# Packed attention and an ELU feed-forward: leftover tokens kept raw, the value product turned, the order set anew

## The chip, the core and the metric

The kernel runs on one core of a Trainium2 chip. The metric is the device time of one execution in microseconds, the median over the timed runs; lower is better.

## The reference

Eight batches of 576 tokens with 8 heads of 64. First 32 packed queries `p` of each head attend to all keys and values; then the 576 queries `q` attend to the 32 packed rows, which serve as keys and as values. The result, 4608 tokens of 512, goes through a feed-forward layer with 2048 hidden units and ELU, all in float32:

```python
p_packed = sm_attn(p, k, v)
out = sm_attn(q, p_packed, p_packed)          # (8, 8, 576, 64) -> x: (4608, 512)
h = x @ w_in
g = np.where(h > 0.0, h, alpha * (np.exp(np.minimum(h, 0.0)) - 1.0))
return (g @ w_out).astype(np.float32)
```

## The kernel before

**Attention of a batch** (`attention`, from line 430). The heads go in four pairs with two heads `g` each; the packed rows of a pair lie in a strip of 32 columns (`cols_of`). TensorE makes the scores (`s1`, L539; L580 in two halves from batch 3 on), DVE takes the row maximum, ACT the exponential with the row sum, and TensorE turns the result 128 columns at a time (`tr1`, L650) so that ACT or DVE can copy it to SBUF as `e1T`. The value product `pv` (L676) then has `e1T` as the stationary operand, 32 columns for each head, and the values, 64 columns, streaming past it; it writes 32 partitions x 64. ACT or DVE scale the rows by the reciprocal sum (`norm`, L688 and L690), TensorE turns the 128x128 result once more (`tr2`, L702), and a copy makes `ppT`, the packed rows with the head dimension on the partitions. `ppT` feeds both the second scores (`s2`, L721) and the products with `w_in` (`mstep`, L822), so that the hidden layer is computed as attention weights times (packed rows times `w_in`).

**Numbers in two words.** A float32 product (L676, L721, L822, L1321) runs in the trace as two passes on TensorE, each with its own load of the stationary operand (PEld) and its own stream (PE). A product of split operands (`a_hi`, `a_lo`, `m_hi`, `m_lo`, `g`, `wo_a`, `wo_b`, `sw`: high word and remainder) is three passes, one for each of three pairings of words, that stream at a faster rate. `H_PLAIN = [0, 1]` lets the first quarter of the hidden layer of batches 0 and 1 use float32 as it is (L1321); all other hidden products are split (L1328, L1059).

**Hidden layer and output.** A batch has two windows of tokens: 256 tokens, and 320 of which 64 are "left over", since output tiles are 128 tokens. ACT makes `relu(-h)` and its exponential, DVE the ELU. The 64 left over tokens of every batch have their ELU made at once (`hb`, written by L1066 and L1344), go to DRAM (`rest_dram`), and are multiplied with `w_out` beside the last batch, 256 of them at a time (`strassen_pair` with `rest`). Batches 0 and 1 go through the output product in `VISITS`, pieces of a window's 16 hidden blocks; each visit ends with two accumulators copied out and stored, added in DRAM by the POOL queue where the rows were stored before. From batch 2 on two hidden blocks are taken together, with Strassen's scheme for the 2x2 blocks: 7 products of 256 columns, 3 passes each (21 passes of L1215), for which DVE makes sums (`sums`, L1141) and weight sums `sw` come from DRAM. `S_PLAINS` names the pairs that are multiplied without it: 4 products of 512 columns, 12 passes of L1215 (where the list of a window lacks pair 0, two of 512 and four of 256, 18 passes).

**What sets the order.** The program is written out by a planner (`schedule`): every piece of work is an `op` with an urgency, a duration for each engine that may do it, the work it needs and the buffers that it takes. The planner goes through time, gives the most urgent ready op to a free engine, and the instructions are then written in that order, one list for each engine. The engines follow their lists, with semaphores for what they need. Where the planner sees TensorE idle in the start-up it puts in matmuls whose result nobody reads (`fill`, L185). Loads are issued by SP's queue in the planned order. `kvq` has two buffers for each batch's keys, values and queries in turn, so that the queries of a batch are loaded once its value product has run.

Of the kernel before, what the change touches and what calls it, by code (L numbers as in the profile page):

```python
# [23 lines left out]
def packed_attention_elu_ffn(  # L24
# [23 lines left out]
    B, P, NPAIR, S = qT.shape  # L48
# [16 lines left out]
    LATE = 1.5  # L65
# [18 lines left out]
    ]  # L84
    T_ATT = [5.5, 0.5, 17.0, 10.0, -5.5, 16.0]
    T_ATT1 = [-22.0, -10.5, -21.5, -13.5, -21.5, -9.0]
    LI = 3.5
    LO = 1.5
    LM = 1.5
    LOOK = 4.0  # L90
    TM = [25.5, 32.5, 37.0, 33.5]
    FIRST = "i2 k q v i1 i3 i0".split()
    T_FILL = 1.5
    T_S2 = -21.0
    STAY = 15
    SWITCH = 0.105
    F_PLAIN = 0
    H_PLAIN = [0, 1]
    T_WS = 7
    T_AS = 3  # L100
# [5 lines left out]
    T_SW7 = 33  # L106
    T_ATTS = {3: [0.5, -1.5, -9.5, -3.0, 11.0, 21.5], 4: [-7.0, 4.5, 13.0, 5.0, 9.5, 23.0], 5: [-5.5, 2, -16.5, -2.5, 12.5, 28.0], 6: [5, 7.5, 13.5, 1.5, 11.5, 24.5], 7: [1.0, -13, 3.0, -3.0, 9.5, 23.0]}
    TMS = {3: [18, 27.0, 35.0, 30.5], 4: [21.5, 19.5, 26.0, 33.0], 5: [12.5, 28.5, 29.0, 29.5], 6: [23, 14.5, 24.0, 27.5], 7: [16.5, 35.5, 32.5, 29.0]}
    T_RL = -3.0
    T_RX = 0.5  # L110
    T_HS = 41.5
    S_FIRST = (2, 0)
    T_SW = 14.0
    T_SL = 6.0
    T_SE = 18.0
    LOOK_S = 5.5
# [70 lines left out]
    def schedule():  # L187
# [8 lines left out]
        todo = sorted(ops, key=lambda o: (o.prio, o.n))  # L196
        idle_at = {e: 0.0 for e in GAP}
        now, out, mode, converted, dense = 0.0, [], None, 0, 0.0
        conv = set(conv_ops)

        def engine_for(o):

            if o.wait or o.ready > now:
# [9 lines left out]
        while todo:  # L213
            for n, o in enumerate(todo[:400]):
                if o.wait or o.ready > now:
                    continue
# [3 lines left out]
                if e == "PE" and o.mode != mode and mode is not None:  # L220

                    for x in todo[n:n + 400]:
                        if x.mode == mode and x.prio < o.prio + STAY and engine_for(x) == "PE":
                            o = x
                            break
# [8 lines left out]
                o.start, o.end = now, now + cost + LAG[e] + o.lag  # L234
                for x, needs in o.next:
                    x.wait -= 1
                    if needs:
                        x.ready = max(x.ready, o.end + x.late)
                for r in {id(b.ring): b.ring for b in o.take}.values():
                    r.take([b for b in o.take if b.ring is r], now)  # L240
                out.append((o, e))
                todo.remove(o)
                converted += o in conv
                break
            else:
                if fill_end.end is None and now >= T_FILL and idle_at["PE"] <= now:
# [11 lines left out]
                    idle_at["PE"] = o.end  # L258
                    out.append((o, "PE"))
                    continue  # L260
                ends = [o.end + t for o, _ in out[-700:] for t in (0, LATE) if o.end + t > now]
                ends += [t for t in idle_at.values() if t > now]
                assert ends, [(o.prio, o.on) for o in todo[:20]]
                now = min(ends)
# [32 lines left out]
    nc.vector.memset(ebias, -1023.0 * LN2)  # L297
    warm = const.tile([P, 1], F32, name="warm")
# [138 lines left out]
    def attention(b, ts):  # L437
# [13 lines left out]
        pp_b = ring_tile("pp", small, [P, G, D], F32, "pp", bufs=1)  # L451
# [25 lines left out]
        def queries(pair, half):  # L477
            if b == 0:
                return q_b[0].t[:, pair, half * HS:(half + 1) * HS]
# [26 lines left out]
        def load_q(e, n):  # L506
            if b == 0:
                nc.sync.dma_start(out=q_b[0].t, in_=qT[b])
            else:
                nc.sync.dma_start(  # L510
                    out=q_b[n].t[:, :NPAIR * HS].rearrange("p (c s) -> p c s", c=NPAIR),
                    in_=qT[b, :, :, n * HS:(n + 1) * HS],
                )

        lds, prev_ld = {}, prev_b and prev_b.ld_q
        for name, fn, bufs, t in (
# [3 lines left out]
            if b == 0:  # L520
                t = FIRST.index(name) - 60
            for n, x in enumerate(bufs):
                prev_ld = op(
                    t, {"DMA": (3.3 if b < 3 else 3.8) / len(bufs)}, lambda e, fn=fn, n=n: fn(e, n),
                    take=[x] + ([p_b] if (name, n) == ("k", 0) else []), after=[prev_ld],
                    lag=1.5 * (b > 2),
# [85 lines left out]
        o4s, o, t, free = [], None, ts[0], prev_b.tmp_last if b > 1 else None  # L612
# [29 lines left out]
        for g in range(G):  # L642
# [23 lines left out]
            tr_done += [o7, o8]  # L666
            e1T.append(eT)
        ps = banks(2)

        def pv(e, ps=ps):  # L670
            for c in range(NKC):
                n = min(P, S - c * P)
                for g in range(G):
                    for pair in range(NPAIR):
                        h = 2 * pair + g
                        nc.tensor.matmul(  # L676
                            ps.t[cols_of(pair), g, :D],
                            lhsT=e1T[g].t[:n, c, cols_of(pair)],
                            rhs=values(c, h)[:n],
                            start=(c == 0), stop=(c == NKC - 1),  # L680
                        )

        o = op(ts[2], {"PE": 1.28}, pv, ld_v + tr_done, take=[ps, pp_b], use=v_b + e1T, mode=2)
        done = []
        for g in range(G):
            def norm(e, g=g, ps=ps):
                if e == "ACT":
                    nc.scalar.mul(pp_b.t[:, g, :], ps.t[:, g, :D], sv["ri"][:, g:g + 1])  # L688
                else:
                    nc.vector.tensor_scalar(  # L690
                        out=pp_b.t[:, g, :], in0=ps.t[:, g, :D], scalar1=sv["ri"][:, g:g + 1],
                        scalar2=None, op0=ALU.mult,
                    )

            done.append(op(
                ts[2], {"ACT": 0.25, "DVE": 0.27}, norm, [o, o5] + done,
                use=[ps, pp_b],
            ))
        pt2 = banks(1)

        def tr2(e, ps=pt2):
            nc.tensor.transpose(  # L702
                out=ps.t[:, :P], in_=pp_b.t.rearrange("p g d -> p (g d)"), identity=ident
            )

        def tr2c(e, ps=pt2):
            copy(e, st.ppT.t.rearrange("p c i -> p (c i)"), ps.t[:, :P])

        o = op(ts[3], {"PE": 0.06}, tr2, done, take=[pt2, st.ppT], use=[pp_b])
        st.ppT_op = op(ts[3], {"ACT": 0.27, "DVE": 0.29}, tr2c, [o], use=[pt2, st.ppT])  # L710
        st.a_done, st.af_done = [], []
        prev = []
        for half in range(2):
# [69 lines left out]
            o = op(t, {"PE": 0.52}, s2, [lds["q"][half % len(q_b)], st.ppT_op],  # L783
# [753 lines left out]
```

## Time and profile before

| | before |
|---|---|
| median of 3 runs | 700.87 us (699.53 to 701.19) |
| profiled execution | 700.24 us, span 698.2 us |
| TensorE busy | 686.1 us, 98% of the span |
| VectorE busy | 573.6 us, 82% |
| ScalarE busy | 455.3 us, 65% |
| granted TensorE clock | 0.998 |
| DMA | 167.80 MB, mean 240 GB/s |

Streams on TensorE overlap at their ends, so one row's duration is longer than the distance to the next row. The chain of waits counts each piece of TensorE work from the start of its first pass to the start of what follows; that is the time that it takes of the engine. "x80" there means 80 passes.

### The profile page before, as it was taken

What the parts mean: (1) busy time and instruction counts of PE and PEld (TensorE: products, weight loads), DVE (VectorE), ACT (ScalarE), POOL (GpSimd) and SP (SyncE); (2) the same over time, 40 slices, a digit from 0 to 9 for tenths busy, and PEclk for the clock granted to TensorE, in tenths of its full rate; (3) what the DMA queues carried; (4) which work ended last, traced back from release to release, by engine and by line L of the source; (5) the groups of instructions that cost most, each with busy time, mean ns of one, the idle gap of its engine ahead of it and who ended that gap; (6) DMA issues with size and microseconds to landing.
All of it is one profiled execution on the core that took longest, in us unless ns stands there. A gap on an engine that the chain in (4) does not pass through costs nothing.

```text
span 698.2 us, 16294 instructions
## 1 busy us (share of the span) xinstructions
PE 686.1 (98%) x6197; PEld 604.8 (87%) x6197; DVE 573.6 (82%) x1282; ACT 455.3 (65%) x888; POOL 21.1 (3%) x30
## 2 busy tenths in 40 slices
PE   8989999999999999999999999999999999999996
PEld 6766878887879989998989988898889988999996
DVE  1989677999978898779977888879978898878874
ACT  4899999775776567665664566665665566555451
POOL 0000011111110000000000000000000000000000
PEclk9999999999999999999999999999999999999999
DMA  9886686889598768687879666797788887675863
GB/s 350 299 286 205 220 230 129 215 224 270 142 255 273 261 216 270 204 263 256 268 260 300 224 228 207 256 296 252 237 275 275 274 260 235 195 215 169 274 222 125
DMA packets 98894, 167.80 MB, mean 240 GB/s; under 512 B 25856, under 2 KB 34048, under 8 KB 98560
## 3 DMA queue, kind: packets, MB, share of 16 engines
q1 hardware_dynamic: 95504, 160.93, 70.6%
q0 software_dynamic: 3168, 5.77, 5.4%
q8 instruction: 49, 0.80, 0.5%
q14 instruction: 29, 0.24, 0.1%
q10 hardware_dynamic: 144, 0.07, 0.0%
HBM read 138.94 MB, written 27.79 MB: 239 GB/s over the span
## 4 chain that ended last, share of the span: by engine, by line
PE 91%; ACT 4%; DVE 2%; DMA 2%; issue 1%; DVEq 0%; SPq 0%; ACTq 0%
PE psum L1215 41%; PE psum L1059 22%; PE psum L822 5%; PE psum L1328 4%; PE psum L1424 3%; PE psum L1425 3%; PE psum L1427 3%; PE psum L185 2%; PE psum L676 2%; PE psum L1321 2%; PE psum L721 1%; PE psum L650 1%; DMA kvq<-in_qT 1%; PE psum L580 1%; DMA k<-in_kT 1%
## 5 line engine op out<-in xcount | busy, mean ns | idle before, releaser
L1215 PE MATMUL psum<-sw,g 128*128 128x256 f32 x1200 | 179.0, 282 | 0.0
L1215 PEld LDWEIGHTS psum<-sw,g 128*128 128x128 f32 x1200 | 157.6, 189 | 7.3 <-issue 4.7
L340 ACT CAST g<-w 128x896 fp32r<-128x896 f32 (+1 forms) x96 | 86.3, 899 | 49.3 <-DVE w L1141 27.8
L1150 DVE TENSOR_TENSOR g<-w,g 128x896 fp32r<-128x896 f32 (+1 forms) x96 | 99.2, 1033 | 23.3 <-ACT g L340 22.6
L1059 PE MATMUL psum<-a_hi,m_hi 128*128 128x256 f32 (+1 forms) x384 | 115.5, 301 | 0.0
L1059 PE MATMUL psum<-a_lo,m_hi 128*128 128x256 f32 (+1 forms) x384 | 113.4, 295 | 0.0
L1059 PE MATMUL psum<-a_hi,m_lo 128*128 128x256 f32 (+1 forms) x384 | 113.4, 295 | 0.0
L1215 PE MATMUL psum<-wo_a,g 128*128 128x256 f32 (+1 forms) x543 | 93.8, 304 | 0.0
L1141 DVE TENSOR_TENSOR w<-w 128x128 f32<-128x128 f32 (+1 forms) x252 | 83.8, 332 | 6.4
L1215 PEld LDWEIGHTS psum<-wo_a,g 128*128 128x128 f32 x543 | 77.9, 189 | 7.0 <-issue 2.6
L1215 PE MATMUL psum<-wo_b,g 128*128 128x256 f32 (+1 forms) x519 | 83.7, 289 | 0.0
L1059 PEld LDWEIGHTS psum<-a_hi,m_hi 128*128 128x128 f32 x384 | 72.7, 189 | 8.8 <-issue 3.2
L1071 ACT ACTIVATE e<-psum 128x320 f32<-128x320 f32 x96 | 41.7, 436 | 59.1 <-PE psum L1059 58.7
L1215 PEld LDWEIGHTS psum<-wo_b,g 128*128 128x128 f32 x519 | 71.5, 189 | 4.9 <-issue 3.9
L1059 PEld LDWEIGHTS psum<-a_lo,m_hi 128*128 128x128 f32 x384 | 72.6, 189 | 0.4
L1059 PEld LDWEIGHTS psum<-a_hi,m_lo 128*128 128x128 f32 x384 | 72.6, 189 | 0.0
L1066 DVE SCALAR_TENSOR_TENSOR w<-e,psum 128x256 f32<-128x256 f32 x96 | 39.8, 415 | 22.2 <-ACT e L1074 21.7
L1071 ACT ACTIVATE w<-psum 128x512 f32<-128x512 f32 x48 | 28.7, 598 | 44.6 <-PE psum L1059 24.8
L1074 ACT ACTIVATE e<-e 128x320 f32<-128x320 f32 x96 | 44.9, 471 | 2.4
L1066 DVE SCALAR_TENSOR_TENSOR w<-w,psum 128x512 f32<-128x512 f32 x48 | 32.5, 678 | 12.6 <-ACT w L1074 12.5
L835 DVE TENSOR_TENSOR m_lo<-psum,m_hi 128x1024 fp32r<-128x1024 f32 (+1 forms) x36 | 37.1, 1038 | 3.7 <-ACT m_hi L340 3.5
L822 PE MATMUL psum<-w_in_sb,ppT 64*32 64x512 f32 (+1 forms) x640 | 35.8, 513 | 0.0
(123 smaller groups left out, 1175.7 us busy)
## 6 DMA issues: line engine op xcount, KB each, us to landing
sw<-sw_dram SPq DMA_DIRECT2D x336, 256.0 KB, 3.7
kvq<-in_v SPq DMA_DIRECT2D x16, 640.0 KB, 6.0
raw<-in_w_in SPq DMA_DIRECT2D x16, 512.0 KB, 4.5
raw<-in_w_out SPq DMA_DIRECT2D x16, 512.0 KB, 4.6
out<-part SPq DMA_DIRECT2D x32, 256.0 KB, 4.4
sw_dram<-sw SPq DMA_DIRECT2D x32, 256.0 KB, 6.3
kvq<-in_kT SPq DMA_DIRECT2D x14, 576.0 KB, 4.9
kvq<-in_qT SPq DMA_DIRECT2D x14, 576.0 KB, 6.0
```

Source lines behind the costliest of these rows:

```text
L340: (nc.scalar.copy if e == "ACT" else nc.vector.tensor_copy)(out=out, in_=in_)
L822: nc.tensor.matmul(ps.t[cols_of(pair), g, :w], lhsT=st.ppT.t[rows_of(g), pair, :], rhs=w_in_sb[rows_of(g), pair, c * FC + part * w:c * FC ...
L835: nc.vector.tensor_tensor(out=m_b[1].t[:, :, fs], in0=ps.t[:, :, :w], in1=m_b[0].t[:, :, fs].bitcast(F32), op=ALU.subtract,)
L1059: nc.tensor.matmul(ps, lhsT=m_b[p].t[:, g, o:o + P], rhs=st.a.t[q][:, g, cols], start=(n == 0), stop=(n == 3 * G - 1),)
L1066: nc.vector.scalar_tensor_tensor(out=out, in0=e_, scalar=-1.0, in1=ps, op0=ALU.add, op1=ALU.max)
L1071: nc.scalar.activation(out=out, in_=ps, func=AF.Relu, scale=-1.0)
L1074: nc.scalar.activation(out=x, in_=x, func=AF.Exp, scale=-1.0)
L1141: nc.vector.tensor_tensor(out=out, in0=x, in1=y, op=o)
L1150: nc.vector.tensor_tensor(out=g_b.all[:, 7 * P:(7 + b1 - b0) * P], in0=blocks(b0, b1), in1=g_b.all[:, :(b1 - b0) * P].bitcast(F32), op=ALU ...
L1215: nc.tensor.matmul(a.t[:, at * H:at * H + rhs.shape[-1]], lhsT=operand(blk, p), rhs=rhs, start=new and n == k == 0, stop=a.final == (u, mi ...
L1328: nc.tensor.matmul(ps_b.t[:, :n_tok], lhsT=m_b[x].t[:, g, o:o + P], rhs=st.a.t[y][:, g, cols], start=(n == 0), stop=(n == 3 * G - 1),)
L1424: nc.tensor.matmul(a.t, lhsT=g_b.t[0][:, t], rhs=wo(f, 0), start=first, stop=False)
```

## The change

1. The value product is turned: the values (64 columns) are the stationary operand, `e1T` (32 columns) streams, and the result is already 64 partitions x 32, the head dimension on the partitions. One op handles one `g`, and all of its 20 products write the same 64 partitions. The second turn (`tr2`) is gone; the row scale is spread over the partitions by `ones` times a diagonal matrix (`diag`, `spread`, `spread_c`) and multiplied in by DVE. 
2. The 64 left over tokens are copied raw from PSUM by ACT or DVE; their ELU is made from `rest_dram` in the last batch (`relu`, `ex`, `elu` on 512 columns).
3. The queries come from memory as two contiguous halves; batch 0 loads them as two transfers.
4. `H_PLAIN` is empty and `S_PLAINS` has 4 pairs in place of 12; 12 visits in place of 15; the urgencies and the planner's window are set anew. At the very end the accumulators are taken in the order 0, 1, 3, 2 and the last store goes out as two halves on two queues.

```diff
     VISITS = [
-        (0, 0, 0, 4), (0, 1, 0, 4), (1, 1, 0, 4), (1, 0, 0, 4),
...
+        (0, 0, 0, 4), (0, 1, 0, 8), (1, 1, 0, 4), (1, 0, 0, 12),
...
-    FIRST = "i2 k q v i1 i3 i0".split()
+    FIRST = "r v k q i3 i1 i2 i0".split()
-    H_PLAIN = [0, 1]
+    H_PLAIN = []
     S_PLAINS = {
-        (2, 0): [0, 7], (2, 1): [0], (3, 0): [1], (3, 1): [0], (4, 0): [0, 4], (4, 1): [1],
-        (5, 0): [0], (5, 1): [0], (6, 0): [0], (6, 1): [7],
+        (2, 0): [], (2, 1): [7], (3, 0): [1, 7], (3, 1): [], (4, 0): [], (4, 1): [],
+        (5, 0): [], (5, 1): [7], (6, 0): [], (6, 1): [],
     }
...
         def load_q(e, n):
             if b == 0:
-                nc.sync.dma_start(out=q_b[0].t, in_=qT[b])
+                x = q_b[0].t.rearrange("p c s -> p (c s)")[:, n * NPAIR * HS:(n + 1) * NPAIR * HS]
             else:
...
+                x = q_b[n].t[:, :NPAIR * HS]
+            nc.sync.dma_start(out=x, in_=qT[b, n].rearrange("p c s -> p (c s)"))
...
-        ps = banks(2)
-
-        def pv(e, ps=ps):
+        ps_v, ps_r = banks(1), banks(1)
+
+        def pv(e, g):
             for c in range(NKC):
                 n = min(P, S - c * P)
-                for g in range(G):
-                    for pair in range(NPAIR):
-                        h = 2 * pair + g
-                        nc.tensor.matmul(
-                            ps.t[cols_of(pair), g, :D],
-                            lhsT=e1T[g].t[:n, c, cols_of(pair)],
-                            rhs=values(c, h)[:n],
-                            start=(c == 0), stop=(c == NKC - 1),
-                        )
-
-        o = op(ts[2], {"PE": 1.28}, pv, ld_v + tr_done, take=[ps, pp_b], use=v_b + e1T, mode=2)
...
+                for pair in range(NPAIR):
+
+                    nc.tensor.matmul(
+                        ps_v.t[rows_of(g), cols_of(pair)], lhsT=values(c, 2 * pair + g)[:n],
+                        rhs=e1T[g].t[:n, c, cols_of(pair)],
+                        start=(c == pair == 0), stop=(c == NKC - 1 and pair == NPAIR - 1),
                     )
...
+        def diag(e, g):
+            out = flat(e1s[1])[:, g * P:(g + 1) * P]
+            if e == "ACT":
+                nc.scalar.mul(out, ident, sv["ri"][:, g:g + 1])
...
+        def spread(e):
+            for g in range(G):
+                nc.tensor.matmul(
+                    ps_r.t[rows_of(g), :P], lhsT=ones, rhs=flat(e1s[1])[:, g * P:(g + 1) * P],
+                    start=True, stop=True,
+                )
...
+        def norm(e):
+            nc.vector.tensor_tensor(
+                out=st.ppT.t.rearrange("p c i -> p (c i)"), in0=ps_v.t[:, :P], in1=pp_b.t, op=ALU.mult
+            )
+
+        o = [op(ts[2], {"PE": 0.64}, lambda e: pv(e, 0), ld_v + tr_done[:2], take=[ps_v], use=v_b + e1T[:1], mode=2)]
...
+        x = op(ts[2], {"PE": 0.26}, spread, ds, take=[ps_r], use=e1s[1:], mode=2)
...
+            x = op(i - T_RE, {"ACT": 0.61}, lambda e: relu(blocks(4, 8), flat_h()), [x], take=[w8], use=[h_b])
+            x = op(i - T_RE, {"ACT": 0.63}, lambda e: ex(blocks(4, 8)), [x], use=[w8])
+            done = [op(
+                i - T_RE, {"DVE": 0.69}, lambda e: elu(blocks(0, 4), blocks(4, 8), flat_h()), [x],
+                use=[w8, h_b],
+            )]
...
                 keep_leftover(b, f + n, op(
-                    i + n + 0.1, {"DVE": 0.21}, lambda e, n=n, ps_b=ps_b, e_b=e_b, l_b=l_b: elu(
-                        l_b.t[:, n, :], e_b.t[:, left], ps_b.t[:, left]
-                    ), [x], **how,
+                    i + n + T_LC, {"ACT": 0.24, "DVE": 0.19}, lambda e, n=n, ps_b=ps_b, l_b=l_b: copy(
+                        e, l_b.t[:, n, :], ps_b.t[:, left]
+                    ), [run["h"]], **how,
                 ), i + n + 0.1)
...
+            def end(e):
+                store(e, 1, slice(0, H))
+                store(e, 1, slice(H, E), nc.scalar)
```

TensorE's list at the value product of batch 4 before: `pv` (L676, 40 products), two hidden blocks' parts (L1059), the second turn (L702).

```order
L1215 MATMUL psum<-sw,g 128x256 x3
L676 MATMUL psum<-kvq,tmp 32x64 x40
L1059 MATMUL psum<-a_hi,m_hi 128x320
L1059 MATMUL psum<-a_lo,m_hi 128x320
L1059 MATMUL psum<-a_hi,m_lo 128x320
L1059 MATMUL psum<-a_hi,m_hi 128x320
L1059 MATMUL psum<-a_lo,m_hi 128x320
L1059 MATMUL psum<-a_hi,m_lo 128x320
L702 MATMUL psum<-ident,pp 128x128
```

The same place of the changed program, in whose numbering L702 is the turned value product, L719 the spread of the row scale, L1092 the hidden product and L1259 the output product:

```order
L1092 MATMUL psum<-a_lo,m_hi 128x320
L1092 MATMUL psum<-a_hi,m_lo 128x320
L702 MATMUL psum<-tmp,kvq 64x32 x20
L719 MATMUL psum<-tmp,ones 64x128 x2
L702 MATMUL psum<-tmp,kvq 64x32 x20
L1259 MATMUL psum<-wo_a,g 128x256 x3
L1259 MATMUL psum<-sw,g 128x256 x9
```

There are 40 products as before, each 64 rows by 32 columns in place of 32 by 64; two spreads came in, the turn went.

ACT's list in the last batch before, one step of it (`kvq` holds the left over tokens here, `w` the batch's own; L340 is the cast to the high word, L1071 and L1074 are the two steps to the ELU):

```order
L340 CAST g<-kvq 128x896
L340 CAST g<-w_9028 128x896
L1071 ACTIVATE w_9197<-psum 128x512
L1074 ACTIVATE w_9197<-w_9197 128x512
L340 CAST g<-kvq 128x896
```

And in the changed program, where they are L365, L1104 and L1107:

```order
L365 CAST g<-kvq 128x896
L365 CAST g<-w_9343 128x896
L1104 ACTIVATE kvq<-tmp 128x512
L1107 ACTIVATE kvq<-kvq 128x512
L1104 ACTIVATE w_9502<-psum 128x512
L1107 ACTIVATE w_9502<-w_9502 128x512
L365 CAST g<-kvq 128x896
```

Two ACT instructions for the left over tokens came into each step; one DVE instruction goes with them.

More of the change, by code (lines that the diff above doesn't have):

```diff
@@ L196, in schedule, with look @@
         todo = sorted(ops, key=lambda o: (o.prio, o.n))
+        for n, o in enumerate(todo):
+            o.at = n
         idle_at = {e: 0.0 for e in GAP}
-        now, out, mode, converted, dense = 0.0, [], None, 0, 0.0
+        now, out, mode, converted, dense, left = 0.0, [], None, 0, 0.0, len(todo)
         conv = set(conv_ops)
+        seen, live, times = 0, [], [0.0]
+        def look():
+            nonlocal seen
+            while seen < len(todo) and seen < LOOK_AT + len(todo) - left:
+                o = todo[seen]
+                seen += 1
+                if not o.wait:
+                    bisect.insort(live, (o.at, o))
         def engine_for(o):
-            if o.wait or o.ready > now:
+            if o.ready > now or min(idle_at[e] for e in o.on) > now:
                 return None
@@ L211, in engine_for @@
             return e if idle_at[e] <= now else None
[L213 to L216, printed above, removed]
+        look()
+        while left:
+            for n, (_, o) in enumerate(live):
                 e = engine_for(o)
@@ L234, in schedule @@
                 o.start, o.end = now, now + cost + LAG[e] + o.lag
+                for t in (idle_at[e], o.end, o.end + LATE):
+                    heapq.heappush(times, t)
+                live.remove((o.at, o))
+                left -= 1
                 for x, needs in o.next:
@@ L238, in schedule @@
                         x.ready = max(x.ready, o.end + x.late)
+                    if not x.wait and x.at < seen:
+                        bisect.insort(live, (x.at, x))
+                look()
                 for r in {id(b.ring): b.ring for b in o.take}.values():
@@ L258, in schedule @@
                     idle_at["PE"] = o.end
+                    heapq.heappush(times, o.end)
                     out.append((o, "PE"))
                     continue
[L261 to L264, printed above, removed]
+                while times and times[0] <= now:
+                    heapq.heappop(times)
+                assert times, [(o.prio, o.on) for _, o in live[:20]]
+                now = times[0]
         return out
@@ L711, in attention @@
+        x = op(ts[2], {"PE": 0.26}, spread, ds, take=[ps_r], use=e1s[1:], mode=2)
+        x = op(ts[2], {"ACT": 0.27, "DVE": 0.29}, spread_c, [x], take=[pp_b], use=[ps_r])
+        o.append(op(
+            ts[2], {"PE": 0.64}, lambda e: pv(e, 1), ld_v + tr_done[2:], use=v_b + e1T[1:] + [ps_v], mode=2,
+            after=o,
+        ))
+        st.ppT_op = op(ts[3], {"DVE": 0.29}, norm, o + [x], take=[st.ppT], use=[ps_v, pp_b])
         st.a_done, st.af_done = [], []
@@ L1208, in strassen_pair @@
             run["pair"] = []
-        for a, group in zip(acc, groups):
+        tail = last and (rest or both)
+        for a, group in [(acc[n], groups[n]) for n in ((0, 1, 3, 2) if tail else range(4))]:
             def mm(e, a=a, group=group, new=not hasattr(a, "last")):
@@ L1516 @@
     arrays = {
-        "in_qT": pairs_T(q),
+        "in_qT": halves(pairs_T(q)),
         "in_kT": pairs_T(k),
```

207 lines of the change are left out of this document (107 added, 100 removed), and 5 rows, old and new, of the table VISITS.

## The prediction

> **What bounds the kernel now.** I read the page first, then TensorE's waits, then the chain of waits.
>
> ```profile
> span 698.2 us, 16294 instructions
> ...
> PE 686.1 (98%) x6197; PEld 604.8 (87%) x6197; DVE 573.6 (82%) x1282; ACT 455.3 (65%) x888; POOL 21.1 (3%) x30
> ...
> PE 91%; ACT 4%; DVE 2%; DMA 2%; issue 1%; DVEq 0%; SPq 0%; ACTq 0%
> ```
>
> The first line is the span, the second the engines' busy time, the third the share of each engine in the chain that ended last. TensorE is busy for all but 12.1 us and is 91% of the chain. DVE, second, has 125 us to spare.
>
> ```profile
> PE psum L721 <- DMA kvq<-in_qT: 2.2, 1, 2.2
> PE psum L185 <- DVE ebias L297: 1.5, 1, 1.5
> PE psum L539 <- DMA k<-in_kT: 0.8, 1, 0.8
> ```
>
> These are TensorE's own waits (total, times, longest). They are small and all in the first 41 us. So a microsecond of TensorE work added or removed is about a microsecond of time, and what other engines get or lose counts only where they fall behind it. The two stretches where that could be are these (start:end, length, then busy PE, PEld, DVE, ACT):
>
> ```profile
> 40.00:120.00 80.00, 78.01 (x530) 59.90 (x531) 62.65 (x144) 77.84 (x178) 5.42 (x6) 1.00 0.74 215
> 640.00:690.00 50.00, 50.00 (x424) 50.00 (x423) 39.08 (x76) 22.41 (x31) 0.00 (x0) 1.00 0.66 213
> ```
>
> From 40 to 120 ACT is as full as TensorE; in the last batch it is not.
>
> **The change, part by part.** The sum is made against the profiled execution, 700.24 us, of which 2.0 lie around the span; the median of the runs is 0.6 above it.
>
> *Output pairs and float32 hidden products.* Rows of the chain of waits (start, time taken, passes), from three stretches:
>
> ```profile
> 208.62 1.39 PE psum L676 x80
> ...
> 211.64 0.11 PE psum L702
> 211.75 2.78 PE psum L1215 x12
> 214.53 1.43 PE psum L1059 x12
> 215.97 2.50 PE psum L1215 x21
> ```
> ```profile
> 25.33 0.86 PE psum L1321 x4
> ```
> ```profile
> 63.28 1.06 PE psum L1321 x4
> ```
> ```profile
> 457.40 0.88 PE psum L1059 x6
> ```
>
> A pair of hidden blocks costs 2.78 with 4 plain products and 2.50 with 7 small ones. Eight pairs go over: 8 x 0.28 = -2.2 us. The hidden products of the 8 short and 8 long blocks that L1321 made take 0.86 (256 tokens) and 1.06 (320 tokens); split, they take 1.43/2 = 0.71 and 0.88: 8 x 0.15 + 8 x 0.18 = -2.6 us. DVE pays for both with sums and remainders, under its spare time.
>
> *The second turn* goes: 8 x 0.11 = -0.9 us. *The spread* comes in: two products of 64 x 128, two passes each. The turn is one pass with a stream of 128, 0.11; if the two halves of the array run abreast it is two such times and a load of 0.05, 0.27 us, if not 0.49. I take 0.27: +2.2 us, with +3.9 as the other end.
>
> *The value product* is the large term. Now it takes 1.39 us for 80 passes, 17.4 ns each. A load of 32 columns alone holds up the next for 26 ns by the rows below, so the passes cannot follow one another; the four pairs write four separate strips of 32 columns (`cols_of`), and run abreast. In the turned form all 20 products of a `g` write the same 64 partitions, so each pass must follow the one before, and what one pass takes is now decided by the longer of its load and its stream. The loads' rows (PEld, partitions*columns of the operand, busy, mean ns):
>
> ```profile
> L1059 PEld LDWEIGHTS psum<-a_hi,m_lo 128*128 128x128 f32 x384 | 72.6, 189 | 0.0
> ...
> L650 PEld LDWEIGHTS psum<-ident,tmp 128*128 128x128 f32 x64 | 7.5, 141 | 1.4 <-ACT tmp L607 0.5 <-ACT top L340 0.4
> L676 PEld LDWEIGHTS psum<-kvq,tmp 128*32 128x32 f32 x512 | 7.5, 110 | 1.4 <-issue 0.4 <-ACT e L1335 0.3
> ...
> L650 PEld LDWEIGHTS psum<-ident,tmp 128*64 128x64 f32 x16 | 1.8, 111 | 0.0
> ```
> ```profile
> 41.47 0.19 PEld L1321 LDWEIGHTS psum<-k,m_hi 128*128 128x128 f32 x1 [0.41 <-issue]
> ```
> ```profile
> 41.58 0.19 PEld L1321 LDWEIGHTS psum<-k,m_hi 128*128 128x128 f32 x1
> ```
> ```profile
> 41.85 0.19 PEld L1321 LDWEIGHTS psum<-k,m_hi 128*128 128x128 f32 x1
> ```
>
> A load of 128 columns lasts 189 ns, one of 32 columns 110: 79 ns for 96 columns, 0.82 ns per column on top of a fixed latency. The last three rows show what part of it blocks the next: after a change of mode the second load starts 0.11 us behind the first (128 columns, 0.86 ns each), while the third comes only when the second stream is let in, 0.27 later. So loads for one place go one behind the other, and one can be made ahead. For 64 columns that is 0.82 to 0.86 x 64 = 53 to 55 ns. The stream is shorter: L676 moves 64 columns in at most 1.39/20 = 70 ns (20 rounds of four abreast), so 32 columns in at most 35. The load sets the pace: 80 x 0.055 = 4.4 us for a batch in place of 1.39, +3.0 each, **+24.1 us** for eight. Each pass of a turn (L650) loads 64 columns faster, (141 - 111)/64 = 0.47 ns per column, 30 ns; that is the nearest row on the other side, and gives 80 x 0.035 = 2.8 us, since the stream then is the longer. I take the first, because L676's load lies on a line with those of all other untransposed products. The lowest end is today's 17.4 ns, +0.
>
> The Trainium skill, page "TensorEngine Tiling (Array Packing)", section "When to Use Tiling", speaks against this edit: where the streamed side has 32 columns or fewer it says to swap the operands, so that four column tiles run side by side, which is the arrangement before. By it alone, with nothing said of loads, four streams in a row in place of abreast would make the term about +9 us; no run here has the turned form.
>
> *Start and waits.* After the value product of batch 1 the queries are loaded into the buffers it frees:
>
> ```profile
> 32.06 1.42 PE psum L676 x80
> 33.48 6.78 DMA kvq<-in_qT
> ```
> ```profile
> kvq<-in_kT SPq DMA_DIRECT2D x14, 576.0 KB, 4.9
> kvq<-in_qT SPq DMA_DIRECT2D x14, 576.0 KB, 6.0
> ```
>
> The keys, as large and contiguous, land in 4.9 us where the queries take 6.0; 6.78 x 4.9/6.0 = 5.5, so the wait of 2.2 falls by 1.2 at the most likely (0 to -2.2). The first keys, and what stands ahead of them on SP's queue, and the last stores:
>
> ```profile
> 0.75 0.39 SPq L367
> ...
> 1.20 6.12 DMA k<-in_kT
> ```
> ```profile
> 693.86 0.84 SPq L1287 DMA_DIRECT2D out<-part x2
> ```
>
> The keys no longer stand behind that weight load's 0.39 us: -0.4. The stores' two issues take 0.84 and the span ends 3.5 us after them; the last one goes out as halves on two queues, one issue less to wait for: -0.4. Both are estimates, bounded by 0 and -1.
>
> *Left over tokens.* In every long block 0.21 us of DVE becomes a copy on ACT or DVE; in the last batch, for each of its 16 pairs of left over blocks, ACT gets two instructions and DVE one:
>
> ```profile
> L1066 DVE SCALAR_TENSOR_TENSOR hb<-e,psum 128x64 f32<-128x64 f32 x96 | 20.5, 213 | 0.2 <-DMA rest_dram<-hb 0.2
> ...
> L1066 DVE SCALAR_TENSOR_TENSOR w<-w,psum 128x512 f32<-128x512 f32 x48 | 32.5, 678 | 12.6 <-ACT w L1074 12.5
> L1074 ACT ACTIVATE w<-w 128x512 f32<-128x512 f32 x48 | 30.4, 634 | 1.1
> ```
>
> In the stretch of 50 us at the end about 8 pairs fall: 8 x 0.68 = 5.4 us on DVE's 39.1, and some 8 x 1.23 = 9.8 on ACT's 22.4. Both stay under 50, so TensorE covers it: 0. What is queued behind these on ACT are the casts of the next operands; if the cover were gone, each step would show ACT's 1.23 us, 16 x 1.23 = 20 us. From 40 to 120 ACT loses six copies of accumulators (three visits fewer) and gains copies of left over tokens; I take 0, between -2.0 (TensorE's idle time there) and +3 (four remainders of 0.69 more on DVE).
>
> Sum: -2.2 - 2.6 - 0.9 + 2.2 + 24.1 - 1.2 - 0.4 - 0.4 = +18.6, 718.8 from the profiled execution; against the median I say **719 us**. Its own range is 714 (all small bounds at their low ends, 53 ns a pass) to 724 (the spread not abreast, +3 in the stretch from 40 on).
>
> **Rivals.**
>
> *The passes stay as quick as today* (faster). Place: the 80 passes of each batch. If the loads of one column half went to both of its strips at once and streams followed without a gap, 17.4 ns could hold. Then the large term is 0 and the rest is left: -5.5, 695 us. The change breaks even at 5.5/640 = 9 ns more, 26 ns a pass. For it: no row shows a load-bound pass. Against: both load rows above.
>
> *The stream, not the load, sets the pace*, 28 (half of a stream of 56) to 35 ns a pass: 2.2 to 2.8 us a batch, +6.8 to +11.3, in all +1.3 to +5.8: about 704. For it: the turns' quick load of 64 columns. Against: those are turns.
>
> *Load and stream do not overlap.* Then a pass is 55 + 28 = 83 ns, 6.6 us a batch, +42 for the term and 737 in all. Against: a pair's 21 passes take 2.50 us, 0.119 each, with 128-column loads of 0.11 under streams of the same order. The Trainium skill, page "TensorE: Matmul & The Clock Gate", section "Part 3: Packing small matmuls — row/col tiling", has a rule of this kind: a load overlaps a running product only in another row group. The trace contradicts it with the 0.119 of L1215.
>
> **How the numbers follow.** Load-bound passes 0.58, as quick as today 0.22, stream-bound 0.15, no overlap 0.05. The range 695 to 724 takes in the first (nearly all), the stream-bound and half of the quick case, about 0.81; the likeliest case alone has 714 to 724. Within 0.3%, about what a measurement of this kernel can tell from no change, is 698.8 to 703.0: half of the stream-bound case, 0.08. Faster is the quick case with the chance of an unforeseen gain, 0.23; slower 0.69.
>
> **What would show it.** In the changed profile the two groups of 40 passes of the turned product in the chain of waits: 2.2 us each if I am right, 0.7 if the quick rival is, 1.1 to 1.4 if the stream sets the pace. Their loads should read about 136 ns. Of the 126 passes of 512 columns in L1215 24 should be left, and no wait of 2.2 for the queries. I am wrong if TensorE's busy time rises by less than 10 us, or if ACT's exponential of left over tokens stands in the chain of the last batch.

## The result

The changed kernel takes 728.35 us (median of 4 runs, 727.82 to 732.05); the kernel before, run beside it, 701.03 (699.53 to 701.46). The ratio on record is 1.0405 with an interval of 1.0367 to 1.0443, which holds the ratio of these medians, 1.039: slower, as forecast, but by 27.3 us where 18.1 were forecast, and above the range's upper end of 724.

The profile after, from its page: the span, the engines' busy times, and the shares of the chain that ended last.

```profile
span 730.3 us, 16714 instructions
...
PE 717.2 (98%) x6333; PEld 641.9 (88%) x6333; DVE 587.9 (81%) x1252; ACT 460.7 (63%) x997; POOL 15.7 (2%) x24
...
PE 75%; DVE 13%; ACT 6%; DMA 3%; issue 2%; DVEq 0%; SPq 0%; ACTq 0%
```

TensorE's busy time has grown by 31.1 us, and the span by 32.1. DVE's share of the chain has gone from 2% to 13%, though it is busy for about the same share of the span as before. The chain of waits at the value product of batch 4 (start, time taken, passes):

```profile
318.23 2.56 PE psum L702 x40
320.79 0.37 PE psum L719 x4
321.16 2.42 PE psum L702 x40
```

L702 is now the value product, L719 the spread. The two halves take 2.56 and 2.42 us; the whole took 1.39 before. The forecast had 2.2 for each half, and 0.27 for the spread. The groups of these lines, and all groups of L1259 (the output products, L1215 before) that stream 512 columns:

```profile
L702 PEld LDWEIGHTS psum<-tmp,kvq 128*64 128x64 f32 (+1 forms) x640 | 41.7, 142 | 2.8 <-DVE w L978 0.4
L702 PE MATMUL psum<-tmp,kvq 128*64 128x32 f32 (+1 forms) x640 | 43.4, 226 | 0.3 <-DMA kvq<-in_v 0.3
```
```profile
L1259 PE MATMUL psum<-wo_b,g 128*128 128x512 f32 x18 | 4.9, 406 | 0.0
...
L1259 PE MATMUL psum<-wo_a,g 128*128 128x512 f32 x6 | 1.5, 393 | 0.0
```

A load lasts 142 ns (136 were forecast), and 18 + 6 = 24 wide passes are left, as forecast. TensorE's waits (total, times, longest):

```profile
PE psum L1092 <- DVE w L1099: 1.9, 2, 1.5
PE psum L1388 <- DVE e L1403: 1.5, 4, 0.5
PE psum L188 <- DVE ones L321: 1.5, 1, 1.5
PE psum L1388 <- DVE m_lo L868: 1.1, 1, 1.1
PE psum L565 <- DMA p<-in_pT: 0.5, 1, 0.5
```

The wait of 2.2 for the queries is gone. New are waits of more than 1 us for DVE in the hidden layer: L1099 is the ELU, L868 the remainder of a split operand.

Adding up, for every pass, the time from its start to the start of the next one gives TensorE's time by kind of work, waits included, up to the start of the last pass (us of the two profiled executions):

| | before | after |
|---|---|---|
| value product | 11.1 | 42.8 |
| spread | 0 | 2.4 |
| turns | 8.3 | 8.1 |
| hidden products | 213.3 | 212.8 |
| output products | 383.4 | 381.8 |
| `w_in` products | 33.5 | 33.5 |
| scores, both | 19.5 | 20.0 |
| filler | 21.7 | 21.5 |

The differences add up to 32.1 us, the whole of the span's growth. The value product holds 31.7 of it. The profiled execution is the longest of the four. A stretch at a halved clock (the last section) makes about 3.1 us of it: 1.6 in the value product, 0.9 in the `w_in` products and 0.6 in the hidden products. The other three executions, with a mean granted clock of 0.998 to 0.999 against 0.993, span 726.0 to 726.7 us.

### The profile page after: what moved, and what is told of

Its sections match the earlier page's. It is cut to its first block, busy times and chain, and to the rows that moved or that the text cites. A ratio compares the mean times of both kernels' runs of the same rounds, so it can differ in the third digit from the quotient of the medians.

```text
span 730.3 us, 16714 instructions
## 1 busy us (share of the span) xinstructions
PE 717.2 (98%) x6333; PEld 641.9 (88%) x6333; DVE 587.9 (81%) x1252; ACT 460.7 (63%) x997; POOL 15.7 (2%) x24
## 3 DMA queue, kind: packets, MB, share of 16 engines
q1 hardware_dynamic: 94880, 169.06, 70.6%
## 4 chain that ended last, share of the span: by engine, by line
PE 75%; DVE 13%; ACT 6%; DMA 3%; issue 2%; DVEq 0%; SPq 0%; ACTq 0%
PE psum L1259 34%; PE psum L1092 20%; PE psum L702 6%; PE psum L855 3%; PE psum L1388 2%; PE psum L188 2%; DMA kvq<-in_v 1%; DVE g L1193 1%; PE psum L1478 1%; ACT top L365 1%; DVE e L1403 1%; DVE g L1412 1%; PE psum L754 1%; PE psum L676 1%; ACT g L365 1%
## 5 line engine op out<-in xcount | busy, mean ns | idle before, releaser
L1259 PE MATMUL psum<-sw,g 128*128 128x256 f32 x1296 | 194.4, 283 | 0.0
L1259 PEld LDWEIGHTS psum<-sw,g 128*128 128x128 f32 x1296 | 170.8, 189 | 8.2 <-issue 3.4
L365 ACT CAST g<-w 128x896 fp32r<-128x896 f32 x96 | 88.8, 925 | 84.3 <-PE psum L1259 42.6
L1092 PE MATMUL psum<-a_hi,m_hi 128*128 128x256 f32 (+1 forms) x384 | 115.8, 301 | 2.4 <-DVE w L1099 1.9
L1193 DVE TENSOR_TENSOR g<-w,g 128x896 fp32r<-128x896 f32 x96 | 102.2, 1066 | 15.3 <-ACT g L365 15.0
L1092 PE MATMUL psum<-a_lo,m_hi 128*128 128x256 f32 (+1 forms) x384 | 113.4, 295 | 0.0
L1092 PE MATMUL psum<-a_hi,m_lo 128*128 128x256 f32 (+1 forms) x384 | 113.4, 295 | 0.0
L1092 PEld LDWEIGHTS psum<-a_hi,m_hi 128*128 128x128 f32 x384 | 72.6, 189 | 13.0 <-issue 4.4
L1259 PE MATMUL psum<-wo_b,g 128*128 128x256 f32 (+1 forms) x531 | 83.1, 286 | 0.0
L1259 PE MATMUL psum<-wo_a,g 128*128 128x256 f32 (+1 forms) x513 | 80.1, 284 | 0.0
L1259 PEld LDWEIGHTS psum<-wo_b,g 128*128 128x128 f32 x531 | 71.9, 188 | 4.9 <-issue 3.5
L1092 PEld LDWEIGHTS psum<-a_lo,m_hi 128*128 128x128 f32 x384 | 72.6, 189 | 0.0
L1092 PEld LDWEIGHTS psum<-a_hi,m_lo 128*128 128x128 f32 x384 | 72.6, 189 | 0.0
L1259 PEld LDWEIGHTS psum<-wo_a,g 128*128 128x128 f32 x513 | 69.7, 189 | 1.6 <-issue 1.3
L1104 ACT ACTIVATE w<-psum 128x512 f32<-128x512 f32 x48 | 28.6, 596 | 45.4 <-PE psum L1092 30.5
L1104 ACT ACTIVATE e<-psum 128x256 f32<-128x256 f32 x96 | 36.3, 381 | 26.5 <-PE psum L1092 21.9
L702 PEld LDWEIGHTS psum<-tmp,kvq 128*64 128x64 f32 (+1 forms) x640 | 41.7, 142 | 2.8 <-DVE w L978 0.4
L702 PE MATMUL psum<-tmp,kvq 128*64 128x32 f32 (+1 forms) x640 | 43.4, 226 | 0.3 <-DMA kvq<-in_v 0.3
L868 DVE TENSOR_TENSOR m_lo<-psum,m_hi 128x1024 fp32r<-128x1024 f32 (+1 forms) x40 | 39.6, 1000 | 5.0 <-ACT m_hi L365 4.8
L365 ACT CAST m_hi<-psum 128x1024 fp32r<-128x1024 f32 (+1 forms) x40 | 33.6, 851 | 15.2 <-PE psum L855 15.0
L1388 PE MATMUL psum<-a_hi,m_hi 128*128 128x256 f32 (+1 forms) x128 | 40.0, 312 | 1.5 <-DVE e L1403 1.5
```

Of the source, the lines that this page charges most:

```text
L365: (nc.scalar.copy if e == "ACT" else nc.vector.tensor_copy)(out=out, in_=in_)
L702: nc.tensor.matmul(ps_v.t[rows_of(g), cols_of(pair)], lhsT=values(c, 2 * pair + g)[:n], rhs=e1T[g].t[:n, c, cols_of(pair)], start=(c == pa ...
L868: nc.vector.tensor_tensor(out=m_b[1].t[:, :, fs], in0=ps.t[:, :, :w], in1=m_b[0].t[:, :, fs].bitcast(F32), op=ALU.subtract,)
L1092: nc.tensor.matmul(ps, lhsT=m_b[p].t[:, g, o:o + P], rhs=st.a.t[q][:, g, cols], start=(n == 0), stop=(n == 3 * G - 1),)
L1104: nc.scalar.activation(out=out, in_=ps, func=AF.Relu, scale=-1.0)
L1193: nc.vector.tensor_tensor(out=g_b.all[:, 7 * P:(7 + b1 - b0) * P], in0=blocks(b0, b1), in1=g_b.all[:, :(b1 - b0) * P].bitcast(F32), op=ALU ...
```

## The experiments

Each ratio is to the kernel before, run beside it on the same chip; in brackets is its 95% interval. The planner writes the order of every kernel anew from its work, so an edit also shifts what stands around it.

**1. The old value product back** (after, with the old `pv`, `norm` and second turn):

```diff
-        ps_v, ps_r = banks(1), banks(1)
-        def pv(e, g): ...
-        def diag(e, g): ...
-        def spread(e): ...
+        ps = banks(2)
+        def pv(e, ps=ps): ...
+        def tr2(e, ps=pt2): ...
```

> The changed kernel with the value product, its scaling and the second turn as they were before (the planner lays the order out anew). If the turned product's own TensorE time is the loss (5.05 us in place of 1.39 for a batch, spread 0.37 in place of a turn of 0.11), 8 x (3.66 + 0.26) = 31 us come back: about 697 us, faster than the kernel before by the pairs and hidden products that are left (-2.2 and -2.6). If the new order, its waits and its transfers are what costs, little comes back: 715 us or more.

709.11 us, 1.0117 [1.0096, 1.0138]. The value product falls back to 11.1 us in all, 1.39 a batch, yet the kernel is not faster than before: undoing the turn gives back 19 us, not 31. Its waits of TensorE:

```profile
PE psum L1382 <- DVE e L1397: 2.6, 5, 1.1
PE psum L1086 <- DVE w L1093: 1.8, 1, 1.8
PE psum L1253 <- DVE w L1093: 1.6, 2, 1.1
```

and two stretches at the start of the last batch (start:end, length, then busy PE, PEld, DVE, ACT, POOL, and the granted clock):

```profile
590.00:600.00 10.00, 8.05 (x60) 7.41 (x59) 9.44 (x22) 5.15 (x10) 0.00 (x0) 1.00 0.68 215
600.00:610.00 10.00, 8.07 (x41) 7.67 (x42) 6.98 (x18) 3.68 (x9) 0.00 (x0) 0.66 0.43 128
```

DVE is full and TensorE is not; in the second stretch the clock is 0.66 as well. The clock is not what makes the time: another execution of this kernel, at a mean clock of 0.999, took 708.95 us. So the rest of the change is not the gain that the forecast made of it.

**2. The turn alone** (before, with the turned value product, the spread and nothing else):

```diff
-        ps = banks(2)
-        def pv(e, ps=ps): ...
+        ps_v, ps_r = banks(1), banks(1)
+        def pv(e, g): ...
+        def diag(e, g): ...
+        def spread(e): ...
```

> The kernel before with the turned value product alone (its spread and scaling too; the planner lays the order out anew). If the passes' own time is the loss whatever the order, 8 x (3.66 + 0.26) = +31 us: about 732 from 701. If a good part of it came with the new order of the changed kernel, clearly less: 720 or under.

736.28 us, 1.0505 [1.0487, 1.0522]: +35.4 us. Its chain of waits at one batch:

```profile
321.52 2.56 PE psum L679 x40
324.08 0.37 PE psum L696 x4
324.45 2.42 PE psum L679 x40
```

The same 2.56, 0.37 and 2.42 with the old order of work: the price does not come from what stands around it. Its eight value products take 40.7 us and the spreads 2.5, less 11.1 before: +32.1. The other 3.3 are in waits, the longest 2.7 for DVE's `m_lo`, and in a stretch of 3.4 us at half the clock from 70.6 on.

**3. A stream twice as long** (after, each pass streams 64 columns; the second 32 belong to the neighbouring pair and nobody reads what they give; the scaling reads the wider result with two DVE instructions):

```diff
-                        ps_v.t[rows_of(g), cols_of(pair)], lhsT=values(c, 2 * pair + g)[:n],
-                        rhs=e1T[g].t[:n, c, cols_of(pair)],
+                        ps_v.t[rows_of(g), pair * 2 * NPK:(pair + 1) * 2 * NPK],
+                        lhsT=values(c, 2 * pair + g)[:n],
+                        rhs=e1T[g].t[:n, c, pair // 2 * 2 * NPK:(pair // 2 + 1) * 2 * NPK],
```

> The changed kernel with each turned product streaming 64 columns, the 32 it needs and 32 that nobody reads; the loads stay 64 columns. If the load sets the pace and the stream (56 ns for 64 columns) goes on under it, the pass stays near 58 ns: 728 to 731. If a pass is load and stream one after the other (58 = 30 + 28), it becomes 85 ns: 640 x 0.027 = +17 us, about 745.

729.22 us, 1.0401 [1.0384, 1.0419], no different from the changed kernel's 1.0405. From its chain:

```profile
315.69 2.61 PE psum L702 x40
...
318.67 2.47 PE psum L702 x40
```

0.05 us more for 40 passes. The longer stream shows only at the start of a half and where the key block changes: the first pass takes 107 ns instead of 79, 28 more for 32 more columns. In a row the passes still start 58 to 59 ns apart. Doubling the stream costs nothing for each pass, so the stream does not set the pace. That the load does is what is left, and the next two kernels test it.

**4. The two halves of the array abreast** (after, both `g` in one op, their passes taken in turn):

```diff
                 for pair in range(NPAIR):
-                    nc.tensor.matmul(
+                    for g in range(G):
+                        nc.tensor.matmul(
...
-        o.append(op(ts[2], {"PE": 0.64}, lambda e: pv(e, 1), ...))
```

> The changed kernel with the turned products of both g in one piece, alternating, so that neighbours write different halves of the array. If a load holds up only loads for the same strip of columns, two passes share each 58 ns: 40 rounds x 0.058 = 2.3 us and a start of 0.2 in place of 5.05, 8 x 2.5 = -20 us, about 708. If a pass of this shape costs 58 ns wherever it goes (a cost of the engine, not of the strip), nothing changes: 728.

715.18 us, 1.0194 [1.0172, 1.0215]. The timeline at the value product of batch 3 (start, duration):

```profile
208.26 2.64 PE L702 MATMUL psum<-tmp,kvq 128*64 128x32 f32 x80
...
210.84 0.50 PE L1474 MATMUL psum<-wo_b,g 128*128 128x512 f32 x1
```

The next work starts 2.58 us after the first pass, about half of 2.56 + 2.42; in a row a pair of passes starts every 58 to 59 ns. So two loads for different halves of the columns go side by side. All eight come to 20.6 us, 22.2 less than in the changed kernel's profile (1.6 of this is its halved clock), but the time falls by only 13, to 715 where 708 were forecast. TensorE now waits for DVE, 2.2 us in the longest group, and the profile has a stretch of 3.4 us at half the clock from 611.8 on; how the rest of the gain is lost in the products around it, no run separates.

**5. Loads of 32 columns, four strips abreast** (after, each head's values in two loads of 32 columns, twice as many passes):

```diff
+                    for j in range(4):
+                        g, d = j // 2, j % 2 * 32
                         nc.tensor.matmul(
-                            ps_v.t[rows_of(g), cols_of(pair)], lhsT=values(c, 2 * pair + g)[:n],
+                            ps_v.t[32 * j:32 * j + 32, cols_of(pair)],
+                            lhsT=values(c, 2 * pair + g)[:n, d:d + 32],
```

> The changed kernel with each turned product cut in two of 32 stationary columns, four strips of the array in turn, both g in one piece: twice the passes, four abreast, each with a load of 32 columns and a stream of 32. If the load sets the pace for each strip by its columns (32 columns 29 ns), it is 40 rounds x 0.030 = 1.2 us and a start, at most 1.5 for a batch: 8 x 3.6 = -29 us, about 699. If load and stream add, or if the engine has a floor per pass, it is 2.3 us or more: 707 or slower.

719.70 us, 1.0262 [1.0233, 1.0291]. From its chain, an undisturbed value product and the next line's start, and then its longest waits:

```profile
214.13 1.68 PE L703 MATMUL psum<-tmp,kvq 128*32 128x32 f32 x160
...
215.74 0.50 PE L1476 MATMUL psum<-wo_b,g 128*128 128x512 f32 x1
```
```profile
PE psum L703 <- issue: 4.6, 2, 2.9
...
PE psum L721 <- issue: 2.2, 1, 2.2
```

160 passes in 1.61 us: at equal work the turned product can come near the old 1.39. In a row four passes, one for each strip, start every 31 to 34 ns, against 58 to 59 for a pass of 64 columns, so the pace follows the columns of the load, about as the expectation had it. In the kernel before, where loads of 32 columns stand under streams of 64, the trace has four passes every 56 ns: there the stream set the pace. But three of the eight batches stall for about 2 to 3 us each on "issue", in which nothing that the profile shows is waited for, two of them after some 120 of the 160 passes and one in the spread behind them, so neither forecast time came. The passes start 8 to 9 ns apart on average; no other kernel here has so many at such distances, and none has a wait of TensorE on "issue".

**6. The old value product with the old plain pairs** (kernel 1, with `S_PLAINS` and `T_SW7` of before):

```diff
-        (2, 0): [], (2, 1): [7], (3, 0): [1, 7], ...
+        (2, 0): [0, 7], (2, 1): [0], (3, 0): [1], (3, 1): [0], ...
-    T_SW7 = 41.5
+    T_SW7 = 33
```

> The run without the turned product (709) with the 12 plain pairs of the kernel before in place of 4. By TensorE's work alone +2.2 us: 711. If DVE's work is what TensorE waits for in that run, the 8 sums saved on DVE (2.1 us each with the longer casts) help more than that: under 708.

707.24 us, 1.0091 [1.0074, 1.0108] against kernel 1's 1.0117 [1.0096, 1.0138]. The intervals overlap, but the 2.2 us that the pairs should cost are excluded. So in this order of work the eight new Strassen pairs bring nothing. That DVE has to make their sums would explain it, but TensorE's waits for DVE, the one at the start left out, only fall from 7.0 us to 6.2, so it is argued and not shown.

**7. The old value product, leftovers' ELU at once again** (kernel 1, with the leftover tokens handled as before):

```diff
-            x = op(i - T_RE, {"ACT": 0.61}, lambda e: relu(blocks(4, 8), flat_h()), ...)
-            x = op(i - T_RE, {"ACT": 0.63}, lambda e: ex(blocks(4, 8)), ...)
-            done = [op(i - T_RE, {"DVE": 0.69}, lambda e: elu(...), ...)]
+                out=blocks(0, 4), in_=rest_dram[b - B, u]...
+            done = [x]
```

> The run without the turned product (709) with the ELU of left over tokens made at once again, as before. That run waited for DVE at the start of the last batch and lost clock there. If the ELU of left over tokens beside the last batch is what DVE is late with, these waits of 4.4 us and the 3.4 us of halved clock go: about 701. If the new order and urgencies make the waits, it stays near 709.

703.57 us, 1.0032 [1.0018, 1.0047]: 0.0085 below kernel 1, 6.0 us. The two stretches of kernel 1, in this kernel:

```profile
590.00:600.00 10.00, 9.76 (x79) 9.55 (x77) 9.72 (x24) 5.43 (x9) 0.00 (x0) 1.00 0.79 247
600.00:610.00 10.00, 9.87 (x79) 9.90 (x80) 6.59 (x17) 4.88 (x9) 0.00 (x0) 1.00 0.86 274
```

TensorE is nearly full again, and the clock with it. Of the 8 us that the expectation wanted back, 6 came.

**8. Raw leftovers alone** (before, with the leftover tokens handled as in the change):

```diff
-            done = [x]
+            x = op(i - T_RE, {"ACT": 0.61}, lambda e: relu(blocks(4, 8), flat_h()), ...)
+            x = op(i - T_RE, {"ACT": 0.63}, lambda e: ex(blocks(4, 8)), ...)
+            done = [op(i - T_RE, {"DVE": 0.69}, lambda e: elu(...), ...)]
```

> The kernel before with the left over tokens kept raw and their ELU done in the last batch, alone. If TensorE covers it, as the prediction had it, 701 within 2 us. If DVE, then at 88% in the last batch (39.1 of 50 us and 5.4 more), comes late at its start, 704 to 709.

706.53 us, 1.0076 [1.0060, 1.0092]: +5.3 us where the forecast had 0. (The profiled execution, 704.49, is the shortest of the four; the others take 706.5 to 706.7.) TensorE's waits for DVE in the last batch, and the two groups on DVE that carry the leftover tokens:

```profile
PE psum L1061 <- DVE m_lo L837: 1.3, 1, 1.3
PE psum L1061 <- DVE w L1068: 1.2, 1, 1.2
```
```profile
L342 DVE COPY hb<-psum 128x64 f32<-128x64 f32 x54 | 12.1, 223 | 22.4 <-ACT e L1073 19.8 <-DMA rest_dram<-hb 0.9 <-DMA sw<-sw_dram 0.7
...
L1068 DVE SCALAR_TENSOR_TENSOR kvq<-kvq,tmp 128x512 f32<-128x512 f32 x16 | 11.0, 689 | 1.3 <-ACT kvq L1076 0.8
```

A copy on DVE takes 223 ns, no less than the ELU that it replaces (213). DVE does 54 copies instead of 128 ELUs, 12.1 instead of 27.3 us, but gets 11.0 us of ELU back, all of it late, and both waits above are at 596 and 599 us, where the last batch begins. In the kernel before, the stretch there reads:

```profile
590.00:600.00 10.00, 10.00 (x82) 10.00 (x81) 9.72 (x25) 5.90 (x10) 0.00 (x0) 1.00 0.55 174
```

TensorE is full and DVE too, with 9.72 of 10 us. The work was moved into a stretch where DVE had hardly any time left.

**9. The changed kernel, leftovers' ELU at once again** (the edit of kernel 7, made to the changed kernel):

```diff
-    T_RL = 11.0
+    T_RL = -3.0
...
-            done = [op(i - T_RE, {"DVE": 0.69}, lambda e: elu(...), ...)]
+            done = [x]
```

> The changed kernel with the left over tokens' ELU done at once again, the turned value product kept. If raw left over tokens cost here what they cost in the kernel before (5.5) and in the one with the old value product (5.5): 728.3 - 5.5 = 723 us. Rival: the longer value products give DVE the time that it lacks, and nothing comes back: 727 to 729 us.

730.03 us, 1.0411 [1.0393, 1.0429]: nothing comes back. With the long value products the raw leftovers cost nothing that can be measured. That DVE makes up time while TensorE is in the value product would explain it; no run shows that directly.

**10. Queries in halves and the new end alone** (before, with the queries of every batch stored as contiguous halves, batch 0's loaded in two parts, and the last adds and stores in the new order):

```diff
-    FIRST = "i2 k q v i1 i3 i0".split()
+    FIRST = "i2 k q r v i1 i3 i0".split()
...
+        tail = last and (rest or both)
...
-        "in_qT": pairs_T(q),
+        "in_qT": halves(pairs_T(q)),
```

> The kernel before with the queries in two halves (second half loaded right behind the first) and with the last two adds and stores in the new order; numbers, pairs, leftovers, value product and turn as before. By the prediction's small terms (queries' wait -1.2, last store -0.4): 701.0 - 1.6 = 699.4 us. Rival: the first wait only moves to the next load, and nothing is gained: 700.5 to 701.5.

700.53 us, 0.9992 [0.9981, 1.0004]: no difference. From its chain, and its waits:

```profile
33.68 6.72 DMA kvq<-in_qT
```
```profile
PE psum L722 <- DMA kvq<-in_qT: 2.9, 2, 2.1
```

The queries of batch 1 take 6.72 us to land as a contiguous half, 6.78 before: the shape of the transfer was not what made it long. In the changed kernel the wait is gone: the queries are asked for at 42.96 us and first used at 48.18, behind 5.1 us of other TensorE work, and the median landing on its profile page is 4.9 us (6.0 before, 7.0 in kernel 10). The new order is what is left to explain it; no run has it alone.

**11. The same, and no float32 hidden products:**

```diff
-    H_PLAIN = [0, 1]
+    H_PLAIN = []
```

> The first kernel of this call with the float32 hidden products of batches 0 and 1 split as well. By the terms: 2.6 less than that kernel, 696.8 us. Rival, ACT and DVE are full there (from 40 to 120 us): no less than that kernel, 699 to 702 us.

706.15 us, 1.0076 [1.0061, 1.0092]: 5.9 us more than kernel 10, where 2.6 less were forecast. One stretch of it:

```profile
60.00:70.00 10.00, 6.70 (x84) 4.68 (x85) 9.76 (x18) 9.72 (x21) 0.00 (x0) 0.78 0.96 353
```

DVE and ACT are full there, TensorE is idle for a third, and the granted clock is 0.78. In kernel 10 the same stretch has TensorE busy for 9.69 us at the full clock:

```profile
60.00:70.00 10.00, 9.69 (x68) 6.67 (x67) 8.39 (x18) 9.97 (x25) 0.00 (x0) 1.00 0.78 255
```

The clock is not the cause: executions of kernel 11 at a mean clock of 0.998 and 0.999 take 705.98 and 705.96 us.

**12. The new pairs and no float32 hidden products, all urgencies as before** (before, with the two tables of the change):

```diff
-    H_PLAIN = [0, 1]
+    H_PLAIN = []
-        (2, 0): [0, 7], (2, 1): [0], ...
+        (2, 0): [], (2, 1): [7], ...
```

> The kernel before with the new table of plain pairs (3 in place of 12 among the Strassen blocks) and no float32 hidden products; everything else and all urgencies as before. By the prediction's terms, TensorE work under DVE's spare time (-2.2 - 2.6): 696.2 us. Rival, as the old pairs in the kernel with the old value product were faster by 2: DVE's added sums are waited for, and as much is given back, 700 to 704 us.

720.26 us, 1.0266 [1.0247, 1.0285], far outside both forecasts. One wait of 6.0 us and the stretch around it:

```profile
PE psum L1215 <- DVE sm L752: 6.0, 1, 6.0
```
```profile
590.00:600.00 10.00, 4.26 (x70) 1.46 (x69) 9.14 (x14) 5.01 (x6) 0.00 (x0) 0.91 0.62 224
```

The softmax of a batch comes late on a DVE that is busy for 9.14 of 10 us. The urgencies here were chosen for the old pairs, so this looks like the price of the new pairs in the old order and not of the pairs themselves: in kernel 7 the same pairs (four in the table; the expectation says three) stand with new urgencies, and cost far less. No run separates the two.

No kernel here is faster than the one before.

## Why the prediction was right and wrong

**The large term: right mechanism, size too small.** Forecast were passes one behind another at the pace of their loads, 55 ns each, 4.4 us a batch. The step that failed here is "80 x 0.055 = 4.4 us": the pace is a little too quick, and the ends of each half are put at nothing. Kernel 3 (stream doubled, same time), kernel 4 (two halves of the columns abreast, half the time), kernel 5 (half the columns, a little over half the distance) and kernel 2 (alone, the same 2.56 and 2.42) show this mechanism. But a batch takes 4.98 to 5.12 us. In the trace the first loads of a half start 55 to 56 ns apart, and the later ones in a row, passes too, 58 to 59 ns: the forecast had the pace of the first loads. That is 640 x 0.003 = 1.9 us. The rest is in the ends of each half: the first pass takes 79 ns, 153 go by where the last 64 of the 576 keys begin (a change from 128 to 64 rows), and about as much at the end. From its first pass to the start of the next work a half is 2.51 to 2.56 instead of 40 x 0.058 = 2.32, so 16 x 0.19 to 0.24 = 3.0 to 3.8 us. Together 5 to 5.7: where no clock drop falls into it (kernels 2, 3 and 9), the term is +29.6 to +30.8, not +24.1. The Trainium skill, page "TensorE: Matmul & The Clock Gate", section "LDWEIGHTS (loading the stationary operand)", would give 64/1.2 = 53 ns for a load (an estimate from its formula); the trace has 55 at first and 58 in a row.

**The spread: nearly right; the turn: too much.** The spread takes 0.37 a batch in the chain, not 0.27 (0.30 by the sum above): +2.4 against +2.2. The second turn was to save 0.9; the time in turns fell by 0.2.

**Pairs and hidden products: the gain did not come.** The step that failed is "DVE pays for both with sums and remainders, under its spare time". The forecast took DVE's 125 us to spare over the whole span as cover in every stretch. TensorE's time in hidden and output products fell by 0.5 + 1.6 = 2.1 us in the changed kernel, or 2.7 without the 0.6 that the halved clock cost the hidden products, not by 4.8. Kernel 7, which has all of the small terms and neither the turned product nor the raw leftovers, should by them be 6.8 us faster than before; it is 2.2 slower. Kernels 6, 11 and 12 have waits for DVE and ACT, and no gain. How much of each is the work and how much the order, they do not separate.

**Queries, first keys, last stores: no gain.** The forecast scaled the queries' landing by the shape of the keys' transfer; kernel 10 shows 6.72 for 6.78. The span ends 5.7 us after TensorE's last pass, 5.6 before, so the new end brought nothing either. The wait for the queries did go in the changed kernel, but other waits came, and the time did not fall with it.

**Leftover tokens: 0 came out by luck.** The step compared DVE's 39.1 + 5.4 with 50 us in the middle of the last batch. The waits of kernel 8 stand at the batch's start, where DVE was already full: 9.72 of 10 us from 590 to 600 in the kernel before. With a short value product the step costs 5 to 6 us (kernels 7 and 8); in the changed kernel it hides (kernel 9). The sentence that would have shown the forecast wrong also came up once, small: ACT's exponential of the leftover tokens stands in the last batch's chain:

```profile
685.01 0.53 ACT kvq L1107
```

**The sum.** Without the 3.1 us of the halved clock the span grew by 29.0 us; the terms add up to 18.6. Of the 10.4 between, 5.9 are in the value product (0.5 of this a wait for the values of batch 2 in its midst), 2.1 in pairs and hidden products (4.8 - 2.7), 0.7 in the second turn and 0.2 in the spread. The remaining 1.4 are what the small terms at both ends lack: they were to save 2.0, and scores, filler and `w_in` products together fell by 0.6. All five lie on one side: costs were taken near their lowest row, gains in full.

**The rivals.** Today's pace, the stream-bound pace and no overlap of load and stream are all excluded, by 17.4, 35 and 83 ns against 58 and by kernel 3. That load and stream overlap also holds against the rule of the Trainium skill that the prediction named: with twice the stream the passes take as long as before.

## What to carry to other kernels

Before two operands of a small product change places, look at which strip of the array's columns each product writes: products that share a strip follow each other at the pace of the load as long as the stream is no longer, here 58 ns for 64 columns, with streams of 32 columns and of 64. When an engine's spare time is to cover added work, read it in the stretch where the work lands, not over the span; DVE was 82% busy in all and 97% where it counted. Where a planner's urgencies were chosen for one set of work, an edit of the work alone can cost more than it was to save: 19.5 us in kernel 12, where 4.8 were to come back.

## What was not expected of the hardware

The granted clock of TensorE can halve in the middle of a kernel in which TensorE is 98% busy. In the changed kernel's profile (start:end, length, busy PE, PEld, DVE, ACT, POOL, clock):

```profile
140.00:143.50 3.50, 3.21 (x56) 3.00 (x48) 3.27 (x7) 1.32 (x3) 0.86 (x1) 1.00 0.88 282
143.50:147.50 4.00, 4.00 (x43) 3.87 (x41) 0.00 (x0) 0.75 (x2) 0.86 (x1) 0.53 0.76 118
147.50:151.00 3.50, 3.50 (x40) 2.27 (x40) 1.18 (x3) 1.48 (x3) 0.00 (x0) 0.57 0.89 274
```

and the chain there:

```profile
143.49 4.06 PE psum L702 x40
```

40 passes take 4.06 us instead of 2.42. Ahead of it TensorE was idle for only 0.3 us, in the midst of passes of 58 ns. In kernel 1 the clock is halved for 6.8 us from 602.2 on, after waits of 0.8 and 1.8. The Trainium skill, page "TensorE: Matmul & The Clock Gate", section "What's actually happening", puts the half rate down to a window of about 3.4 us without activity; 6.8 is two of these, but the longest wait in the 14 us ahead of either drop is 1.8, so the trace does not bear out a whole window without work. Kernel 3 has as many passes in the same place, after a wait of 0.2, and no drop. And the changed kernel itself, the same program, ran three more times at a mean clock of 0.998 to 0.999, which leaves no room for such a drop. So what tips it stays open.

Loads and streams for different strips of columns cost nothing extra side by side: 58 ns for one pass of 64 columns, 58 for two in different halves, and 31 to 34 for four of 32 columns. At that last rate, though, TensorE stood still for about 2 to 3 us in three of eight batches without a wait that the profile shows (kernel 5); the cause is open.
